# Experts half a step further behind the attention, first gate's sums by one-column matmuls, orders from token lists

## The chip, the cores and the metric

The kernel runs on one core of one Trainium2 chip. The metric is device time in microseconds (us) of one execution. Medians are over all timed runs of a kernel. A ratio is the mean time of one kernel's fast runs over the mean of the other's fast runs in the same rounds, so it is not quite the ratio of the medians. The profile of a kernel is one execution with the hardware profiler; its span is about 1.6 us shorter than the device time of the same run. The two executions compared stage by stage below, before and after, are both some 2 us slower than the medians of their kernels (241.70 against 239.66 us, 247.45 against 245.39).

Engine names in the profile: PE is TensorE, DVE VectorE, ACT ScalarE, POOL GpSimd, SP SyncE, which issues most loads and stores.

## The reference

Eight batches, eight heads, 576 positions, head size 64. Causal attention with a bias from a running sum of `s`; its output `x` (576 x 512 per batch) goes to a mixture of eight experts, of which one is chosen for a whole batch by the mean of `x`.

```python
scores = scale * np.matmul(q, k.transpose(0, 1, 3, 2))
cum = np.cumsum(np.maximum(s, 0.0), axis=-1)
bias = -(cum[:, :, :, None] - cum[:, :, None, :])
scores = np.where(causal, -1e9, scores + np.minimum(bias, 0.0))
attn = softmax(scores)                        # written out in the reference
x = np.matmul(attn, v)                        # then heads side by side: (8, 576, 512)
pooled = x.mean(axis=1)
logits = pooled @ w_gate                      # (8, 8)
e_idx = np.argmax(logits, axis=1)
h = np.maximum(x[mask] @ w1[e], 0.0)          # for each expert e and its batches
out[mask] = gate_w[mask, None, None] * (h @ w2[e])
```

The weights of an expert (two matrices of 512 x 1024) can be asked for only when the gate has chosen it.

## The kernel before

The attention is cut into 32 units of two heads, four to a batch. Two units share one load group of q, k and v. The experts' matmuls of a batch fill TensorE between the attention steps of later batches. The order on every engine is the order in which Python emits the instructions. Before, a hand-written function emits the start, and a loop with budgets the rest. The parts that matter:

```python
def load(n, after=None):          # SyncE's queue: q, k, and v in five pieces per group
    ...
def cast_qk(n, i):                # VectorE: q (i=0) or k (i=1) of group n to bf16
    ...
        nc.vector.tensor_copy(out=qk_bf[n][...], in_=src...)
def do_vS_pair(n, g):             # GpSimd: v of two heads, scaled by a column
    ...
    nc.gpsimd.tensor_tensor(out=dst[...], in0=src[...], in1=gc[...], op=ALU.mult)

def do_x(b, c):                   # transpose a quarter of x; copy it out with its sum
    ...
        nc.scalar.activation(out=xT[b][:, c, :], in_=flat, func=AF.Copy,
                             accum_out=pooled[b][:, c : c + 1])
    ...                           # or the same on VectorE; then gate_part(b, c - 1)

def do_gate(b):
    nc.tensor.matmul(lp, ones_sq, glog[b], start=True, stop=True)
    ...                           # VectorE: largest of eight, its index
    e_val = nc.gpsimd.value_load(idxc[0:1, 0:1], min_val=0, max_val=E - 1)
    picked[b] = nc.gpsimd.dma_start(out=w1, in_=moe_w1[e_val]...)
    nc.gpsimd.dma_start(out=w2, in_=moe_w2[e_val]...)

def begin():
    ...
    do_av_part(3, 0); do_av_part(3, 1)
    cast_qk(3, 0)
    do_tr_part(2, 1, 0, "a")
    for c in range(NC):
        do_x(0, c)
    do_tr_part(2, 1, 1, "a")
    do_gate(0)
    do_tr_part(3, 0, 0, "v")
    do_vS_pair(2, 0); do_vS_pair(2, 1)
    load(5, picked[0]); load(6)
    do_scores_masked(4, 0); exp_only(4, 0)
    do_gate2(0)
    cast_qk(3, 1)
    ...
    do_vS(3)
```

At the end `do_guard()` computes a flag on VectorE and TensorE (whether a general path is needed), every engine reads it and branches on it.

Of the kernel before, what the change touches and what calls it, by code (L numbers as in the profile page):

```python
# [9 lines left out]
FP32 = mybir.dt.float32  # L10
# [7 lines left out]
P = 128  # L18

# [248 lines left out]
def kernel(  # L268
# [11 lines left out]
    nc = tc.nc  # L280
# [36 lines left out]
    NQT, NPT, NVS, NVN = 2, 3, 2, 4  # L317
    NEARLY = 4
# [10 lines left out]

    def load_qk(n, i, after=None):  # L330
        b, Q = divmod(n, NQ)
        if i == 0:
            qk_nat[n] = nat.tile([P, 2, 2, R * D], FP32, name="qk_nat")
        ld = nc.sync.dma_start(
            out=qk_nat[n][:, i, :, :],
            in_=(q, k)[i][b, 4 * Q : 4 * Q + 4].rearrange(
                "(hh g) (p r) d -> (g p) hh (r d)", hh=2, p=64
            ),
        )
        if after is not None:  # L340
            tc.add_manual_dep(
                ld.ins, after.ins.name,
                mybir.DependencyInfo(mybir.DependencyClass.Sync, mybir.DependencyReason.DATA),
                reason="the weights of the chosen expert go first",
            )

    vS_done = set()

    def load_v(n, hh, eng=nc.sync):
        b, Q = divmod(n, NQ)  # L350
        assert n < NVN or n - NVN in vS_done
# [12 lines left out]
    def load(n, after=None):  # L364

        rest = n > 1 and after is None
        rest = rest and n > 2
        if n == 2:
            for m in range(2):
                for hh in range(5):  # L370
                    load_v(m, hh)
        if after is not None:
            for hh in (2, 3, 4):
                load_v(n - 1, hh)
        load_qk(n, 0, after)
        if rest:
            load_v(n - 1, 2)
            load_v(n - 1, 3)
        load_qk(n, 1)
        if rest:  # L380
            load_v(n - 1, 4)
        if n == NB - 1:
            for hh in range(5):
                load_v(n, hh)
        elif n > 1:
            load_v(n, 0)
            load_v(n, 1)

    def cast_qk(n, i):

        src = qk_nat[n][:, i, :, :]
        if n < NEARLY:
# [6 lines left out]
        if i == 0:  # L399
            qk_bf[n] = natb.tile([P, 2, R, 2, D], BF16, name="qk_bf")  # L400
# [11 lines left out]
    def do_tr_part(n, i, part, eng):  # L412
        r0, r1 = ((0, 5), (5, R))[part]
        tr = ps_mm.tile([P, 8, P], BF16, name="tr_ps", tag="mm_ps")
        for r in range(r0, r1):
            nc.tensor.transpose(tr[:, r - r0, :], qk_bf[n][:, i, r, :, :], ident_bf)  # L416
        o = tr_out(n, i, r0, r1)
        src = tr[:, 0 : r1 - r0, :].rearrange("p r (g n) -> p g n r", g=2)
        if eng == "v":
            nc.vector.tensor_copy(out=o, in_=src)  # L420
        else:
            nc.scalar.copy(out=o, in_=src)  # L422

    def do_tr(n, i):
        tr = ps_att.tile([P, 2, 8, P], BF16, name="tr_ps", tag="att_b")
        flat = tr.rearrange("p k r m -> p (k r) m")
        for r in range(R):
            nc.tensor.transpose(flat[:, r, :], qk_bf[n][:, i, r, :, :], ident_bf)  # L428
        j = 4 * n + 2 * i
# [4 lines left out]
        )  # L434

    def do_vS(n):
        b, Q = divmod(n, NQ)
        vS_done.add(n)
# [8 lines left out]
    def do_vS_pair(n, g):  # L447
        b, Q = divmod(n, NQ)
        src, dst = vN[n % NVN], vS[n % NVS]
        if g == 1:  # L450
            vS_done.add(n)
# [11 lines left out]
    def do_scores_half(u, half, alone=True):  # L463
        n, g = divmod(u, 2)
        src = qkT[n % NQT]
# [33 lines left out]
    def exp_only(u, half):  # L499
        ph = pT[u % NPT][:, 2 * half * HALF : 2 * (half + 1) * HALF]  # L500
        nc.scalar.activation(out=ph, in_=sc_ps[half], func=AF.Exp, scale=SCALE)  # L501
        return ph

    def do_exp(u, half):
        ph = exp_only(u, half)
# [12 lines left out]
    x_nat = {}  # L518

    def av_mm(u, hh, av):  # L520
        src = pT[u % NPT]
# [14 lines left out]
    def x_home(u):  # L536
        b = u // NC
        if b not in x_nat:
            x_nat[b] = xpool.tile([P, NT, H, D], BF16, name="x_nat", bufs=2)
        return x_nat[b], 4 * (u // 2 % NQ) + u % 2  # L540

    def do_av_part(u, hh):
        av = ps_mm.tile([P, NT, D + 1], FP32, name="av_ps", tag="mm_ps")
        av_mm(u, hh, av)
# [8 lines left out]
        )  # L553

    def do_av(u):
        av = ps_att.tile([P, 2, HALF], FP32, name="av_ps", tag="att_a")
        a4 = av[:, :, 0 : NT * (D + 1)].rearrange("p k (t d) -> p k t d", d=D + 1)
        for hh in range(2):
            av_mm(u, hh, a4[:, hh, :, :])
# [8 lines left out]
        )  # L568

# [3 lines left out]
    def do_x(b, c):  # L573
        if c == 0:
            xT[b] = xpool.tile([P, NC, S], BF16, name="xT", bufs=2)
            pooled[b] = small.tile([P, NC], FP32, name="pooled")
        src = x_nat[b].rearrange("p t h d -> p t (h d)")
        tr = ps_mm.tile([P, 8, P], BF16, name="x_ps", tag="mm_ps")
        for t in range(NT):
            nc.tensor.transpose(tr[:, t, :], src[:, t, c::NC], ident_bf)  # L580
        flat = tr.rearrange("p t n -> p (t n)")[:, 0:S]
        if c % 2 == 0 or b > 0:
# [8 lines left out]
        if c > 0:  # L591
            gate_part(b, c - 1)
        if c == NC - 1:
            gate_part(b, c)
# [6 lines left out]

    def gate_part(b, c):
        if c == 0:
# [10 lines left out]
    def do_gate(b):  # L614

        lp = ps_mm.tile([P, E], FP32, name="lg_ps", tag="mm_ps")
        nc.tensor.matmul(lp, ones_sq, glog[b], start=True, stop=True)  # L617
# [18 lines left out]
    def do_gate2(b):  # L636
# [12 lines left out]
    def do_mm1(b, sc, ft):  # L649
        if b not in hT:  # L650
            hT[b] = hpool.tile([P, NF, SP], BF16, name="hT")
        w1 = w_sb[b][0].rearrange("p c (m f) -> p c f m", f=NF)
        mm = ps_mm.tile([P, SC], FP32, name="mm_ps")
        for c in range(NC):
# [3 lines left out]
            )  # L658
        dst = hT[b][:, ft, sc * SC : (sc + 1) * SC]
        if RELU[ft] == "v":  # L660
            nc.vector.tensor_scalar_max(out=dst, in0=mm, scalar1=0.0)  # L661
        else:
            nc.scalar.activation(out=dst, in_=mm, func=AF.Relu)  # L663

    def do_mm2_tail(b, mm):
        w2 = w_sb[b][1]
        for fc in range(NF):
# [8 lines left out]
        o = opool.tile([P, Dm], FP32, name="o_sb")  # L676
        nc.scalar.mul(o[:, 0 : Dm // 2], mm[:, 0 : Dm // 2], gate[b])
        stores.append((b, NT - 1, TAIL, o))

    mm2_ps = {}  # L680
    stores = []

    def do_mm2(b, st, part):
        w2 = w_sb[b][1]
        n = min(P, S - st * P)
        if part == 0:
            mm2_ps[b, st] = ps_mm.tile([P, Dm], FP32, name="mm_ps")
        mm = mm2_ps[b, st]
        if st == NT - 1:
            do_mm2_tail(b, mm)  # L690
            return
        for fc in range(part * NF // 2, (part + 1) * NF // 2):
            nc.tensor.matmul(  # L693
                mm[0:n, :], hT[b][:, fc, st * P : st * P + n], w2[:, fc, :],
                start=(fc == 0), stop=(fc == NF - 1),
            )
        if part == 1:
            o = opool.tile([P, Dm], FP32, name="o_sb")
            if OEV[st] == "v":
                nc.vector.tensor_scalar_mul(out=o[0:n, :], in0=mm[0:n, :], scalar1=gate[b][0:n, :])  # L700
            else:
                nc.scalar.mul(o[0:n, :], mm[0:n, :], gate[b][0:n, :])  # L702
            stores.append((b, st, n, o))

    def do_store(all_=False):
        while stores and (all_ or len(stores) > 1):
            b, st, n, o = stores.pop(0)
            if st == NT - 1:
                for j in range(2):
                    nc.sync.dma_start(  # L710
                        out=out[b, st * P : st * P + n, j * Dm // 2 : (j + 1) * Dm // 2],
                        in_=o[j * 64 : j * 64 + n, 0 : Dm // 2],
                    )
                continue
            nc.sync.dma_start(out=out[b, st * P : st * P + n, :], in_=o[0:n, :])

    RELU = "avavavav"
    OEV = "aaaaa"

    def moe_quanta(b):  # L720
        q1 = [(1, partial(do_mm1, b, sc, ft)) for sc in range(2) for ft in range(NF)]
        q2 = [(1.76, partial(do_mm2, b, st, part)) for st in range(NT) for part in range(2)][:-1]

        return q1[0:9] + q2[0:2] + q1[9:11] + q2[2:4] + q1[11:] + q2[4:]


    s_nat = consts.tile([BH, S], FP32)
    nc.sync.dma_start(out=s_nat, in_=s.rearrange("b h i -> (b h) i"))
    for n in range(4):
        load(n)  # L730
    w_gate_sb = consts.tile([P, NC, E], FP32)
    nc.gpsimd.dma_start(out=w_gate_sb, in_=moe_w_gate.rearrange("(p c) e -> p c e", c=NC))

# [11 lines left out]
    )  # L745
    ones_sq = consts.tile([P, P], FP32)
# [21 lines left out]
    def do_gcol():  # L768
        g_ps = ps_mm.tile([P, NT, BH], FP32, name="mm_ps")
# [8 lines left out]
    NU = NC * B  # L778
    LAG = 7
    BEGIN = [LAG, LAG + 3] + [NC * b + LAG for b in range(2, B)]  # L780
    END = NU + LAG
    PRE = 3
    KEEP0 = 11

    def keep_pe(cnt):

        t = ps_mm.tile([P, 512], FP32, name="mm_ps")
# [3 lines left out]
    def early_max(n):  # L791
        nc.vector.tensor_reduce(
# [4 lines left out]
    def begin():  # L797
        keep_pe(KEEP0)
        cast_qk(0, 0)
        do_tr_part(0, 0, 0, "a")  # L800
        do_tr_part(0, 0, 1, "a")
        keep_pe(2)
        cast_qk(0, 1)
        do_tr_part(0, 1, 0, "v")
        do_gcol()
        do_tr_part(0, 1, 1, "a")
# [201 lines left out]
```

## Time and profile before

| before | value | how to read it |
|---|---|---|
| device time | 239.66 us, median of 3 (238.68 to 244.06) | later rounds on the other chips gave medians of 239.7 to 240.5 |
| span of the profile | 240.1 us, TensorE busy 214.1 | TensorE is the bound; its gaps are the question |
| gates (start of the gate matmul) | 27.11, 51.08, 80.58, 106.55, 132.30, 158.54, 183.38, 205.17 us | the distances are the periods |
| first expert matmul, last expert matmul's end | 39.41 and 233.69 us | between them TensorE is almost full |
| tail | 6.42 us | from the last matmul to the end |

To compare two kernels stage by stage I use one more mark: the first scores that follow the first attention product, at 16.37 us here. What comes before it is mostly the first loads, whose landing differs from run to run (the first q lands at 5.7 to 7.3 us in the fourteen profiles).

### The profile page before, as it was taken

Reading aid. Unit: us, or ns where it says so; the run is one execution under the profiler, and the core shown is the slowest. Engines: PE = TensorE matmul, PEld = TensorE weight load, DVE = VectorE, ACT = ScalarE, POOL = GpSimd, SP = SyncE. Lnnn points to the kernel's source line nnn. Section 1 sums busy time; section 2 is a strip of 40 time slices with the busy share of each in tenths; the row PEclk is TensorE's granted clock in tenths of the full one; section 3 lists DMA queues with packets and bytes.
Section 4 is the critical chain, followed back from the end, with each engine's and each line's share of the span. In section 5 each row is a group of like instructions: output and inputs, shape, how many; then the busy total and the mean of one; then the engine's idle time right before and its main releaser. Section 6 shows DMA issues by size and latency. Waiting matters only on the chain.

```text
span 240.1 us, 5998 instructions
## 1 busy us (share of the span) xinstructions
PE 214.1 (89%) x2330; PEld 157.1 (65%) x2330; DVE 164.5 (69%) x378; ACT 140.3 (58%) x254; POOL 92.6 (39%) x145
## 2 busy tenths in 40 slices
PE   6597789999999796999899997999999998898990
PEld 2365457875787655867597857776877776557740
DVE  5578768658797784779686875777777544396640
ACT  2588547467656745576648655685658675434330
POOL 6181092018845194308362556218360830100000
PEclk9999859999999999999999999999999999999997
DMA  5999999999999999999999999969921893399222
GB/s 174 342 237 351 306 200 216 344 309 284 221 309 312 286 257 209 304 306 305 225 254 347 313 217 241 337 159 187 228 94 44 162 230 117 67 214 235 82 84 76
DMA packets 55186, 55.14 MB, mean 230 GB/s; under 512 B 39712, under 2 KB 40752, under 8 KB 53104
## 3 DMA queue, kind: packets, MB, share of 16 engines
q1 hardware_dynamic: 52816, 37.91, 51.8%
q0 software_dynamic: 2336, 16.79, 35.4%
q8 instruction: 20, 0.33, 0.5%
q14 instruction: 14, 0.11, 0.2%
HBM read 62.03 MB, written 9.44 MB: 298 GB/s over the span
## 4 chain that ended last, share of the span: by engine, by line
PE 52%; DMA 26%; ACT 7%; DVE 7%; issue 4%; POOLq 1%; SPq 0%; ACTq 0%; POOL 0%; DVEq 0%
DMA w_sb<-in_moe_w_dram 24%; PE mm_ps L655 18%; PE mm_ps L693 13%; PE av_ps L528 6%; PE sc_ps L471 4%; ACT xT L583 4%; PE tr_ps L428 3%; DMA qk_nat<-in_k_dram 2%; ACT pT L501 2%; PE x_ps L580 2%; PE sc_ps L488 1%; PE tr_ps L416 1%; PE lg_ps L617 1%; PE mm_ps L669 1%; POOLq L624 1%
## 5 line engine op out<-in xcount | busy, mean ns | idle before, releaser
L655 PE MATMUL mm_ps<-xT,w_sb 128*128 128x288 bf16 x512 | 74.5, 289 | 4.9 <-DMA w_sb<-in_moe_w_dram 4.4
L501 ACT ACTIVATE pT<-sc_ps 128x1024 bf16<-128x1024 f32 x64 | 62.5, 1021 | 23.5 <-PE sc_ps L471 14.7
L655 PEld LDWEIGHTS <-w_sb 128*128 128x128 bf16 x512 | 61.5, 146 | 9.0 <-DMA w_sb<-in_moe_w_dram 5.1
L693 PE MATMUL mm_ps<-w_sb,hT 128*128 128x512 bf16 x256 | 64.9, 380 | 1.3 <-DMA w_sb<-in_moe_w_dram 0.6
L507 POOL TENSOR_SCALAR_AFFINE_SELECT pT<-pT 128x512 bf16<-128x512 bf16 x50 | 31.5, 638 | 43.8 <-ACT pT L501 43.7
L661 DVE TENSOR_SCALAR hT<-mm_ps 128x288 bf16<-128x288 f32 x64 | 28.7, 454 | 22.0 <-PE mm_ps L655 22.0
L663 ACT ACTIVATE hT<-mm_ps 128x288 bf16<-128x288 f32 x64 | 26.4, 413 | 26.8 <-PE mm_ps L655 26.1
L702 ACT ACTIVATE o_sb<-mm_ps,gw 128x512 f32<-128x512 f32 x32 | 22.1, 691 | 31.2 <-PE mm_ps L693 31.1
L693 PEld LDWEIGHTS <-hT 128*128 128x128 bf16 x256 | 22.8, 98 | 22.1 <-DVE hT L661 2.9
L430 DVE TENSOR_SCALAR_CACHE_REDUCE qkT<-tr_ps 128x1152 bf16<-128x1152 bf16 x24 | 32.5, 1353 | 3.8 <-PE tr_ps L428 3.6
L401 DVE TENSOR_SCALAR_CACHE_REDUCE qk_bf<-qk_nat 128x1152 bf16<-128x1152 f32 x24 | 32.1, 1342 | 0.0
L441 POOL TENSOR_TENSOR vS<-vN,g_col 128x1280 bf16<-128x1280 f32 x13 | 30.3, 2332 | 0.0
L626 POOL DMA_DIRECT2D w_sb<-in_moe_w_dram x8 | 5.2, 645 | 63.1 <-issue 18.7
L528 PEld LDWEIGHTS <-pT 128*128 128x128 bf16 x576 | 22.4, 99 | 4.7 <-ACT pT L501 1.4
L528 PE MATMUL av_ps<-vS,pT 128*128 128x65 bf16 x576 | 23.8, 195 | 1.1 <-ACT pT L501 0.9
L471 PE MATMUL sc_ps<-qkT 64*128 64x256 bf16 (+2 forms) x320 | 21.7, 256 | 1.8 <-ACT qkT L422 1.1
L563 DVE TENSOR_TENSOR x_nat<-av_ps,recip 128x640 bf16<-128x640 f32 x26 | 21.4, 824 | 0.9
L583 ACT ACTIVATE xT<-x_ps 128x576 bf16<-128x576 bf16 x30 | 19.2, 650 | 3.4 <-PE x_ps L580 3.0
L471 PEld LDWEIGHTS <-qkT 64*128 64x128 bf16 x320 | 12.6, 95 | 11.2 <-issue 3.9
L428 PE MATMUL tr_ps<-ident_bf,qk_bf 128*128 128x128 bf16 x216 | 16.0, 219 | 0.1
L428 PEld LDWEIGHTS <-qk_bf 128*128 128x128 bf16 x216 | 13.9, 98 | 3.1 <-DVE qk_bf L401 0.5
L561 DVE RECIPROCAL recip<-av_ps 128x10 f32<-128x10 f32 x26 | 5.7, 220 | 14.0 <-PE av_ps L528 12.9
(92 smaller groups left out, 187.8 us busy)
## 6 DMA issues: line engine op xcount, KB each, us to landing
w_sb<-in_moe_w_dram POOLq DMA_DIRECT2D x16, 1024.0 KB, 12.4
qk_nat<-in_q_dram SPq DMA_DIRECT2D x16, 576.0 KB, 5.6
qk_nat<-in_k_dram SPq DMA_DIRECT2D x16, 576.0 KB, 6.3
vN<-in_v_dram SPq DMA_DIRECT2D x64, 128.0 KB, 5.5
out_dram<-o_sb SPq DMA_DIRECT2D x32, 256.0 KB, 5.7
vN<-in_v_dram SPq DMA_DIRECT2D x16, 64.0 KB, 5.8
out_dram<-o_sb SPq DMA_DIRECT2D x16, 64.0 KB, 4.2
s_nat<-in_s_dram SPq DMA_DIRECT2D x1, 144.0 KB, 2.8
```

Of the source, the lines that this page charges most:

```text
L401: nc.vector.tensor_scalar(out=qk_bf[n][:, i, :, :, :].rearrange("p r hh d -> p hh r d"), in0=src.rearrange("p hh (r d) -> p hh r d", d=D), ...
L428: nc.tensor.transpose(flat[:, r, :], qk_bf[n][:, i, r, :, :], ident_bf)
L430: nc.vector.tensor_scalar(out=tr_out(n, i, 0, R), in0=flat[:, 0:R, :].rearrange("p r (g n) -> p g n r", g=2), scalar1=1.0, scalar2=0.0, op ...
L441: nc.gpsimd.tensor_tensor(out=dst[:, :, :, 0:D], in0=src, in1=gc[:, :, :, None].to_broadcast([P, NT, 4, D]), op=ALU.mult,)
L471: nc.tensor.matmul(sc[:, hh, o : o + W[tj]], src[hh * 64 : hh * 64 + 64, 1, g, tj * P : tj * P + P], src[hh * 64 : hh * 64 + 64, 0, g, tj ...
L501: nc.scalar.activation(out=ph, in_=sc_ps[half], func=AF.Exp, scale=SCALE)
L507: nc.gpsimd.affine_select(out=ap, in_=ap, compare_op=ALU.is_ge, fill=0.0, base=0, pattern=[[0, 4], [1, P]], channel_multiplier=-1,)
L528: nc.tensor.matmul(av[:, ti, :], src[:, o : o + P], vs[:, tj, 2 * hh + u % 2, :], start=(tj == tjs[0]), stop=(tj == tjs[-1]),)
L583: nc.scalar.activation(out=xT[b][:, c, :], in_=flat, func=AF.Copy, accum_out=pooled[b][:, c : c + 1])
L655: nc.tensor.matmul(mm, w1[:, c, ft, :], xT[b][:, c, sc * SC : (sc + 1) * SC], start=(c == 0), stop=(c == NC - 1),)
L661: nc.vector.tensor_scalar_max(out=dst, in0=mm, scalar1=0.0)
L693: nc.tensor.matmul(mm[0:n, :], hT[b][:, fc, st * P : st * P + n], w2[:, fc, :], start=(fc == 0), stop=(fc == NF - 1),)
```

## The change

Its intent: the experts of a batch start half a step later, so that more work stands between a gate and the first matmul that needs its weights; the first gate gets its sums of x from matmuls with a column of ones straight after the attention, without waiting for the x transposes and their copies; and every engine's order comes from lists of tokens, tuned by hand at the fine joints. One token is one helper call: `C3.1` casts k of group 3, `v2.0` scales half of the v of group 2, `V3` all of group 3, `l3.4` loads a v piece, `G0 m0` are the first gate's matmul and pick, `D` is the guard.

```diff
+BEGIN = """
+k2 k11 C0.0 U0.0.0 u0.0.0.1 ... C1.0 v0.0 v0.1 l3.2 L4.0 l3.3 L4.1 l3.4 l4.0 l4.1 U1.0.0 ...
+... B2.0 b2.0 B2.1 b2.1 N0 n0 N1 n1 M3.1 E3.1
+U2.0.0 u2.0.0.1 U2.0.1 u2.0.1.1 C2.1 B3.0 b3.0 B3.1 b3.1 N2 N3 n2 n3 X0.0 x0.0.1 G0 m0 C3.0 X0.1
+U2.1.1 u2.1.1.1 x0.1.0 X0.2 x0.2.1 U2.1.0 u2.1.0.1 l4.4 X0.3 x0.3.0 U3.0.0 u3.0.0.0 v2.0 v2.1
+l4.2 l5.0 l5.1 l4.3 W5.0 l6.1 M4.0 g0 L5.1 l5.3 L6.0 l5.4 L6.1 E4.0 l6.0 l5.2 C3.1 U3.0.1
+u3.0.1.0 M4.1 E4.1 U3.1.0 u3.1.0.1 U3.1.1 u3.1.1.0 V3 M5.0 ...            (cut)
+"""
+PERIOD = ...   # one batch's tokens, played four times, shifted by one batch
+FINISH = """   ... Y7.3.0 Y7.3.1 y7.3.1 Z7 y7.4.2 O7.3 O7.4.2 D
+"""
-    def begin():  ...          # and the loop with budgets
-    def do_x(b, c):
+    def x_mm(b, c):            # every helper split into its TensorE part and its way out
+    def x_out(b, c, eng):
+        if b == 0:             # first batch: a plain copy, no sum
+            ...
+    w_gate_n = consts.tile([P, NC, E], FP32)
+    nc.scalar.dma_start(out=w_gate_n, in_=moe_w_gate.rearrange("(c p) e -> p c e", p=P))
+    def sum_mm(j):             # the sums of 128 channels over 576 positions
+        for ti in range(NT):
+            nc.tensor.matmul(t, src[0:n, ti, j * P : (j + 1) * P], ones_bf[0:n, :],
+                             start=(ti == 0), stop=(ti == NT - 1))
```

The sums come out with channels in another order than the old ones, so the gate's table is loaded a second time (`w_gate_n`). In the old order the guard stood inside the last second-layer product, `Y7.3.0 D Y7.3.1`.

## The prediction

> **What bounds the kernel now.** I read the page first, then the PE waits, then the timeline at each of those waits, then the chain, then the end of the span.
>
> ```profile
> PE 214.1 (89%) x2330; PEld 157.1 (65%) x2330; DVE 164.5 (69%) x378; ACT 140.3 (58%) x254; POOL 92.6 (39%) x145
> ...
> PE   6597789999999796999899997999999998898990
> ...
> PEclk9999859999999999999999999999999999999997
> DMA  5999999999999999999999999969921893399222
> ```
>
> PE is the bound: 26 us of its span are idle, and they lie in a few places. From 0 to 38 us it is 6 to 9 tenths busy. The clock row falls to 8 and 5 tenths around 24 to 36 us. Between 38 and 234 us PE is nearly full, with dents. The last 6.4 us have no matmul. These are the dents:
>
> ```profile
> PE mm_ps L655 <- DMA w_sb<-in_moe_w_dram: 4.4, 4, 2.1
> PE lg_ps L617 <- DVE glog L609: 3.0, 3, 1.4
> PE x_ps L580 <- DVE x_nat L563: 0.7, 1, 0.7
> PE sc_ps L471 <- DVE qkT L430: 0.6, 2, 0.4
> PE mm_ps L693 <- DMA w_sb<-in_moe_w_dram: 0.6, 1, 0.6
> PE mm_ps L693 <- DVE hT L661: 0.3, 1, 0.3
> ```
>
> That view covers 37 to 234 us and sums to 9.6 us; half is the first expert matmul of a batch waiting for weights that were asked for only when the gate had chosen the expert. The timeline gives the places:
>
> ```profile
> 80.58 0.39 PE L617 MATMUL lg_ps<-glog,ones_sq 128*128 128x8 f32 x2 [1.37 <-DVE glog L609]
> 94.08 1.20 PE L655 MATMUL mm_ps<-xT,w_sb 128*128 128x288 bf16 x8 [2.06 <-DMA w_sb<-in_moe_w_dram]
> 119.83 1.20 PE L655 MATMUL mm_ps<-xT,w_sb 128*128 128x288 bf16 x8 [0.84 <-DMA w_sb<-in_moe_w_dram]
> 146.07 1.20 PE L655 MATMUL mm_ps<-xT,w_sb 128*128 128x288 bf16 x8 [1.33 <-DMA w_sb<-in_moe_w_dram]
> ```
>
> Gate to weights takes 13.45 us for batch 2 (80.58 to 94.03). By the same reading of the chain it is 13.2 us for batch 3 and 13.7 us for batch 4. Batches 5 and 6 do not wait, because the loads are over and the DMA row falls to 6 tenths and below. The steady period between gate matmuls is 25.75 us (gate 3 to 4), 26.24 us (4 to 5) and 24.84 us (5 to 6); the last has no weight wait and is the floor of this order.
>
> The first gate is slow too, and the end of the span holds a wait that is not on the page's engine rows:
>
> ```profile
> 27.11 0.36 PE L617 MATMUL lg_ps<-glog,ones_sq 128*128 128x8 f32 x2 [1.50 <-DVE glog L609]
> ...
> L976 PEldq COMPARE_BRANCH  x1: 4102/4102/4102, 233.7 to 233.7; - x1
> L976 SPq COMPARE_BRANCH  x1: 50/50/50, 236.5 to 236.5; - x1
> ```
>
> The second pair is the branch on the guard's flag (whether the general path runs). PE's takes 4.10 us, from 233.7 to 237.8. It costs nothing now, since SP waits for the last store until 237.88 anyway and then needs 2.2 us to the end.
>
> [...] Here PE idles 0.69 and 1.50 us around the first gate among short transposes, and the clock drops for about 6.8 us[...]. [...] the chain gives it, 10.64 us from issue to landing for batch 2, of which the 2.1 MB read as f32 would take 7 us alone at the profile's 298 GB/s.
>
> **The change part by part.** Order alone carries no new bytes. I rebuilt both kernels' instruction orders and compared them engine by engine. Unit costs on PE, from start to start in the chain: one expert step H (4 matmuls of 288 columns) 0.49 us, half a second-layer tile Y 0.86, a tail Z 0.99, scores S 0.55, attention-value A 0.55, transposes T 0.50, one x transpose 0.28.
>
> 1. Start. Before, the first gate needs four x transposes, four evacuations with sums (0.65+0.20 us each on ACT, 0.75+0.08 on DVE) and four gate sums. Now sums of x come from 4 groups of 5 one-column matmuls; I take each as a transpose-like 0.06 to 0.1 us, for its weight load, so 0.3 to 0.5 us a group. Two groups come before attention unit 3 and delay it by up to 0.8 us less one filler; two follow it. Last x slice ready 23.9 us, + 0.8 delay + 0.5 (last group) + 0.5 (two DVE steps) + 0.1 = 25.8 against 27.1. First weights then land at 36.6 instead of 37.9. [...] But ACT must still do the x copies, two qkT copies and seven exponentials of 1.02 us before unit 7, about 11 us from 25.3, so the first expert starts near 37 to 38.5 instead of 39.4. Gain 1.5 us (0.5 to 2.5).
>
> 2. Batch 2. After its gate, PE now has 5H+5Y+2S+3A+2T+Z = 11.5 us of work before its first expert matmul, against 4H+4Y+3S+2A+2T+Z = 10.2. The gate's own wait shrinks because a score and a Y half (1.4 us) stand before it: 1.37 to about 0.8. A new wait of about 1 us appears at unit 14's scores, which now follow their transposes after 0.5 us while DVE needs 1.35. Together: 2.0 us gained.
>
> 3. Batches 3 to 6. After the gate PE has 6H+5 or 6Y+3S+3A+2T+Z, about 13.4 us, against 11.5 before (12.0 measured with joints, so 14.0 now). Weights need 13.2 and 13.7, so both waits go: 0.84 and 1.33. The 0.27 us joint at L693 <- DVE hT in each period goes too. The x transposes get new small waits (0.2 and 0.3 us, PSUM buffers freed by ACT in order) in place of the old 0.29 and 0.18. Period 24.5 us: 1.2 + 1.7 + 0.3 = 3.2 us gained.
>
> 4. DVE. Per period three 512-column evacuations and one x evacuation move to it (3 x 0.69 + 0.83) and three hT ones leave (3 x 0.45): 19.3 + 1.5 = 20.9 us of 24.5. It stays under PE.
>
> 5. Batch 7. The x wait (0.65) goes, as three H stand there. The gate's wait grows from 1.45 to about 2 us, since DVE carries hT and two x evacuations in series. The wait for second weights (0.65, at 221.8) goes, as 17.8 us of work stands behind the gate where 15.4 stood. The guard's transposes leave the middle of the last tile (0.4). Sum 1.8 us with joints.
>
> 6. Tail. The guard now comes last on DVE and PE. From the last matmul, T: evacuation to T+0.5, guard's first DVE part 0.8, transposes 0.7, second part 1.3, flag read 0.5: T+4.0. PE's branch of up to 4.1 us then starts after, not before, the stores: T+8.2, and 1.0 us to the end, T+9.2. SP's way: flag ready T+3.5, read and checked 1.1, at least 0.5 past the branch, 2.2 to the end as now, so T+7.3 at the earliest. Now it is T+6.4. Cost 1.0 to 2.8 us, taken as 2.0. Splitting the last store over two queues saves 0.5 us that no longer sets the end.
>
> Sum: 1.5 + 2.0 + 3.2 + 1.8 + 0.1 (batch 1) - 2.0 = 6.6 us off 239.66, so 233.0 us.
>
> **The rivals.** (a) The weights merely wait elsewhere: loads are regrouped, DMA is full until 145 us, and a gate that comes sooner meets the same queue. For it: 10.6 us under load against 8.3 to 8.7 for batches 5 to 7. Against: the extra 1.9 us of work exceeds the wait. If weights took 2 us more, steps 2 and 3 lose 3 us: 236. (b) DVE or ACT becomes the bound through in-order evacuation: DVE at 85% of a period with 4 PSUM buffers leaves little slack. Half a us per period and some at the ends: 236 to 238. (c) The tail eats more or nothing: [...] if it is the whole 4.1 us, 234. (d) Fine-grained orders remove joints that my sums leave alone, and the clock stays up at the start: 229 to 231.
>
> **Range and chances.** 233.0 us, 229.0 to 237.0 eight times in ten. Two per cent is 234.9. The centre is beyond it by 1.9 us with a spread of about 3, and a deliberate order is more likely to help than my added waits: faster 0.70, same 0.27, slower 0.03.
>
> **What would show it.** Step 1: first gate matmul near 25.8 us, first expert matmul at 37 to 38.5, clock slices without a 5. Step 2 and 3: PE <- DMA w_sb waits under 1.5 us in sum, gate-to-gate periods near 24.5 us. Step 4: DVE about 21 us per period. Step 5: gate 7 still waits about 2 us for DVE. Step 6: span minus last expert matmul 7.3 to 9.2 us, with PE's branch after the guard. Periods above 25.2 us, or new PE waits on DVE over 3 us in sum, would prove the sum wrong; so would a tail still at 6.4.

## The result, and the profile after

The changed kernel took 245.39 us (median of 4, 245.27 to 247.45) against 239.73 (4 runs, 238.68 to 244.06) in the same rounds: ratio 1.027, interval 1.021 to 1.033. It is slower. All runs of the changed kernel were in the fast state.

Stage by stage, in us, from the two traces:

| stage | before | after | after less before | predicted |
|---|---|---|---|---|
| start to the mark | 16.37 | 16.39 | 0.0 | 0 |
| mark to second gate | 34.71 | 43.38 | +8.7 | -1.6 |
| second gate to last gate | 154.09 | 148.47 | -5.6 | -5.2, and a part of step 5 |
| last gate to last matmul | 28.52 | 28.56 | 0.0 | the rest of step 5's -1.8 |
| tail | 6.42 | 8.99 | +2.6 | +2.0 |
| span | 240.1 | 245.8 | +5.7 | -6.6 |

The middle did nearly what was hoped. The whole loss is in the start, and a smaller one in the tail. The rows of the page of the changed kernel that answer to the first fence of the prediction:

```profile
PE 213.9 (87%) x2326; PEld 159.9 (65%) x2350; DVE 173.8 (71%) x392; ACT 130.0 (53%) x238; POOL 90.9 (37%) x145
...
PE   7787773599899897999999999999999997999950
...
PEclk9999998589999999999999999999999999999997
DMA  5999999984999969999999999999940992597140
```

A slice is 6.1 us. TensorE does the same work (213.9 us busy), but slices 7 and 8 (37 to 49 us) are 3 and 5 tenths busy, and the clock falls to 5 tenths in and behind the hole (in the trace it is at half from 40.8 to 51.0 us). From 49 us on there are hardly any dents. The waits of TensorE from 48 to 238 us (waited for; us in total, times, longest) no longer hold one for expert weights:

```profile
PE sc_ps L567 <- DVE qkT L518: 1.6, 2, 1.4
PE lg_ps L784 <- DVE glog L746: 1.6, 1, 1.6
PE tr_ps L511 <- DVE qk_bf L471: 0.9, 1, 0.9
```

Before, `w_sb` stood at the top of that view with 4.4 us. The same view from 20 to 48 us shows the new ones:

```profile
PE av_ps L633 <- POOL vS L537: 7.0, 1, 7.0
PE tr_ps L490 <- DVE early L463: 2.6, 1, 2.6
```

In the timeline of TensorE of the changed kernel (start, us, engine, line, operation; in brackets the idle time before it and what ended it):

```profile
25.03 0.39 PE L784 MATMUL lg_ps<-glog,ones_sq 128*128 128x8 f32 x2
...
32.19 0.68 PE L490 MATMUL tr_ps<-ident_bf,early 128*128 128x128 bf16 x9 [2.61 <-DVE early L463]
...
45.80 1.15 PE L633 MATMUL av_ps<-vS,pT 128*128 128x65 bf16 x18 [6.96 <-POOL vS L537]
46.76 5.43 PE L831 MATMUL mm_ps<-xT,w_sb 128*128 128x288 bf16 x26
```

The gate came 2.1 us sooner than before (27.11), as it should. The first expert matmul came 7.4 us later (39.41 before). Between them stand two waits, one for GpSimd and one for VectorE.

**The long wait.** GpSimd's timeline of the changed kernel:

```profile
27.61 0.59 POOL L797 DMA_DIRECT2D w_sb<-in_moe_w_dram  x1 [8.78 <-DVE xT L717]
...
28.89 1.27 POOL L549 TENSOR_TENSOR vS<-vN,g_col 128x640 bf16<-128x640 f32 x1
...
30.26 1.25 POOL L549 TENSOR_TENSOR vS<-vN,g_col 128x640 bf16<-128x640 f32 x1
43.20 2.33 POOL L533 TENSOR_TENSOR vS<-vN,g_col 128x1280 bf16<-128x1280 f32 x1 [11.69 <-DMA vN<-in_v_dram]
```

The scaling of group 3's v (`V3`) waited 11.7 us for a v piece. SyncE issued that piece, `l3.4`, at 26.81 us, 0.8 us ahead of the weights. The trace records its landing in sixteen shares, which I take for one share per DMA engine (the page counts 16). Fifteen of them had landed by 32.6 us; the last landed at 43.04, and the last packet of the weights ended at 42.59. In the kernel before, the piece was issued at 25.96 us and landed at 32.06, with the weights issued only at 29.67, and GpSimd did the same scaling at 34.07 without a wait:

```profile
34.07 2.33 POOL L441 TENSOR_TENSOR vS<-vN,g_col 128x1280 bf16<-128x1280 f32 x1
```

The kernel before had trapped pieces too: the v pieces issued at 28.75 and 31.00 us landed at 44.48 and 44.83, but nothing waited for them. What the change moved is which piece is in the trap.

The view of the DMA of the changed kernel from 33 to 41 us (queue: packets, MB, share of the 16 engines' time; then the issues of the window, with the median time to landing) shows what the piece was up against; the v pieces it lists are later ones, the last of them issued at 28.99 us:

```profile
q0 software_dynamic: 214, 1.62, 96.8%
q1 hardware_dynamic: 214, 0.05, 5.0%
...
vN<-in_v_dram SPq DMA_DIRECT2D x2, 128.0 KB, 5.3
vN<-in_v_dram SPq DMA_DIRECT2D x1, 64.0 KB, 14.9
```

q0 carries the weights, q1 everything of SyncE. Both moved 214 packets, and in each of the eight microseconds the two counts differ by at most one (22 to 36 packets each): the engines took one of each in turn. A packet of the weights is 8 KB and took 624 ns in the trace, one of v is 256 bytes and took 31 (medians; 16 of the 214 on q0 carry 4 bytes). So q1 had half of the turns and a thirtieth of the bytes. The piece, 64 KB in packets of 256 bytes, has 16 packets for each engine if the shares are equal. My estimate for an engine that has all 16 left when the weights arrive is 16 x 0.65 = 10.4 us, and the difference between 32.6 and 43.0 is as much. The packed trace does not keep which engine a packet ran on, so that the late engine had all of them left is inferred.

**The short wait.** A cast on VectorE, of k of group 3, in the changed kernel (second line; the first is the q cast just ahead of it):

```profile
26.15 0.74 DVE L463 CAST early<-qk_nat 128x1152 bf16<-128x1152 f32 x1
28.56 3.57 DVE L463 CAST early<-qk_nat 128x1152 bf16<-128x1152 f32 x1
```

and the same cast in the kernel before:

```profile
29.93 0.74 DVE L394 CAST early<-qk_nat 128x1152 bf16<-128x1152 f32 x1
```

The same work took 3.57 us instead of 0.74. In the changed kernel it lay beside GpSimd's two scalings (28.89 to 31.51 us) and ended 0.6 us after them. Before, GpSimd was issuing the weights during the cast and scaled afterwards. In GpSimd's timelines, the weight issue during which the cast starts, before and then changed:

```profile
29.67 1.12 POOL L626 DMA_DIRECT2D w_sb<-in_moe_w_dram  x1 [10.57 <-DVE qkT L420]
28.20 0.54 POOL L799 DMA_DIRECT2D w_sb<-in_moe_w_dram  x1
```

Before, it was thus the issue that took longer (1.12 us, where the median of the eight is 0.58). In all five traces in which the cast starts 0.24 to 0.27 us into a weight issue (before, e4, e7, e8, e10 below), that issue takes 1.1 us and the cast 0.74; in the three in which it starts 0.35 to 0.37 us into one (changed, e1, e2), the issue takes 0.54 and the cast waits for all the scalings. About a tenth of a microsecond separates the two groups. Which was first in the changed kernel the trace does not settle: the cast is recorded at 28.56 us, inside GpSimd's second weight issue (28.20 to 28.74) and ahead of its first scaling (28.89). Nor does it show by what means the one holds the other; it shows the two times, 0.74 against 3.57 us.

**The tail.** The branch on the guard's flag, in the view of its source line (engine, operation, count, duration in ns, first and last start):

```profile
L1020 SPq COMPARE_BRANCH  x1: 50/50/50, 241.0 to 241.0; - x1
...
L1020 PEldq COMPARE_BRANCH  x1: 3582/3582/3582, 241.1 to 241.1; - x1
```

The guard's last VectorE step ended at 240.46 us, 3.7 us after the last expert matmul; then TensorE's branch took 3.58 us. The stores had landed by 239.8. So the guard and the branch set the end, where before the last store did.

### The profile page after: what moved, and what is told of

Same layout as the page of the kernel before. It is cut to its first block, busy times and chain, and to the rows that moved or that the text cites. A ratio compares the mean times of both kernels' runs of the same rounds, so it can differ in the third digit from the quotient of the medians.

```text
span 245.8 us, 6001 instructions
## 1 busy us (share of the span) xinstructions
PE 213.9 (87%) x2326; PEld 159.9 (65%) x2350; DVE 173.8 (71%) x392; ACT 130.0 (53%) x238; POOL 90.9 (37%) x145
## 3 DMA queue, kind: packets, MB, share of 16 engines
q0 software_dynamic: 2336, 16.79, 34.6%
## 4 chain that ended last, share of the span: by engine, by line
PE 68%; DVE 11%; DMA 9%; ACT 3%; issue 3%; SPq 2%; POOL 1%; ACTq 0%; DVEq 0%
PE mm_ps L831 23%; PE mm_ps L863 20%; PE av_ps L633 6%; DMA vN<-in_v_dram 6%; PE sc_ps L567 6%; PE tr_ps L511 4%; PE x_ps L708 3%; DVE x_nat L684 3%; PE mm_ps L892 3%; DMA qk_nat<-in_k_dram 2%; ACT pT L599 2%; DVE qkT L518 2%; DVE qk_bf L471 1%; POOL vS L533 1%; SPq L446 1%
## 5 line engine op out<-in xcount | busy, mean ns | idle before, releaser
L831 PE MATMUL mm_ps<-xT,w_sb 128*128 128x288 bf16 x512 | 77.0, 295 | 0.0
L831 PEld LDWEIGHTS <-w_sb 128*128 128x128 bf16 x512 | 62.5, 147 | 5.3
L863 PE MATMUL mm_ps<-w_sb,hT 128*128 128x512 bf16 x234 | 59.2, 379 | 1.2 <-issue 0.2
L841 ACT ACTIVATE hT<-mm_ps 128x288 bf16<-128x288 f32 x77 | 29.7, 415 | 38.1 <-PE mm_ps L831 37.1
L606 POOL TENSOR_SCALAR_AFFINE_SELECT pT<-pT 128x512 bf16<-128x512 bf16 x50 | 31.5, 638 | 38.5 <-ACT pT L599 38.4
L863 PEld LDWEIGHTS <-hT 128*128 128x128 bf16 x256 | 23.5, 98 | 22.3 <-issue 1.1
L843 DVE TENSOR_SCALAR hT<-mm_ps 128x288 bf16<-128x288 f32 x51 | 22.3, 451 | 18.8 <-PE mm_ps L831 18.8
L533 POOL TENSOR_TENSOR vS<-vN,g_col 128x1280 bf16<-128x1280 f32 x13 | 30.4, 2337 | 11.7 <-DMA vN<-in_v_dram 11.7
L633 PEld LDWEIGHTS <-pT 128*128 128x128 bf16 x576 | 22.4, 98 | 11.7 <-issue 6.7
L797 POOL DMA_DIRECT2D w_sb<-in_moe_w_dram x8 | 4.6, 577 | 61.7 <-issue 21.1
L879 ACT ACTIVATE o_sb<-mm_ps,gw 128x512 f32<-128x512 f32 (+1 forms) x25 | 15.6, 628 | 12.5 <-PE mm_ps L863 7.8
L719 ACT ACTIVATE xT<-x_ps 128x576 bf16<-128x576 bf16 x21 | 13.5, 649 | 7.1 <-PE x_ps L708 7.1
L881 DVE TENSOR_SCALAR o_sb<-mm_ps,gw 128x512 f32<-128x512 f32 x14 | 10.4, 744 | 9.5 <-PE mm_ps L863 9.5
```

Source lines behind the costliest of these rows:

```text
L533: nc.gpsimd.tensor_tensor(out=dst[:, :, :, 0:D], in0=src, in1=gc[:, :, :, None].to_broadcast([P, NT, 4, D]), op=ALU.mult,)
L606: nc.gpsimd.affine_select(out=ap, in_=ap, compare_op=ALU.is_ge, fill=0.0, base=0, pattern=[[0, 4], [1, P]], channel_multiplier=-1,)
L633: nc.tensor.matmul(av[:, ti, :], src[:, o : o + P], vs[:, tj, 2 * hh + u % 2, :], start=(tj == tjs[0]), stop=(tj == tjs[-1]),)
L831: nc.tensor.matmul(mm, w1[:, c, ft, :], xT[b][:, c, sc * SC : (sc + 1) * SC], start=(c == 0), stop=(c == NC - 1),)
L841: nc.scalar.activation(out=dst, in_=mm, func=AF.Relu)
L863: nc.tensor.matmul(mm[0:n, :], hT[b][:, fc, st * P : st * P + n], w2[:, fc, :], start=(fc == 0), stop=(fc == NF - 1),)
```

## The experiments

Theory: (1) the early weights trap the v piece, (2) the cast is blocked by GpSimd's scaling, (3) the late guard lengthens the tail. The rival to (1) and (2) is that only the half step and the other new orders make the start later. Twelve kernels ran. Every edit is to the changed kernel unless said otherwise, and all gave correct results. This table is from their profiles, in us:

| run | time, median | ratio to before | mark | mark to 2nd gate | 2nd to last gate | last gate to last matmul | tail |
|---|---|---|---|---|---|---|---|
| before | 239.7 | | 16.4 | 34.7 | 154.1 | 28.5 | 6.4 |
| after | 245.4 | 1.027 | 16.4 | 43.4 | 148.5 | 28.6 | 9.0 |
| e1_v3_first | 244.4 | 1.020 | 17.1 | 39.5 | 148.5 | 28.6 | 9.1 |
| e2_guard_early | 240.6 | 1.000 | 17.2 | 36.9 | 148.5 | 29.0 | 6.2 |
| e3_gate_late | 239.9 | 0.998 | 18.6 | 33.6 | 148.5 | 28.6 | 9.1 |
| e4_old_start | 241.5 | 1.004 | 18.2 | 35.5 | 149.0 | 28.6 | 9.1 |
| e5_late_guard | 237.2 | 0.988 | 18.8 | 33.7 | 148.5 | 29.0 | 6.1 |
| e6_v3_cast | 240.5 | 1.002 | 19.0 | 33.2 | 150.1 | 28.6 | 9.3 |
| e7_before_list | 242.2 | 1.010 | 19.4 | 33.8 | 152.9 | 28.6 | 6.6 |
| e8_before_sums | 240.7 | 1.002 | 18.1 | 34.2 | 151.7 | 28.4 | 6.5 |
| e9_late_table | 237.3 | 0.987 | 16.1 | 36.3 | 148.1 | 29.0 | 6.2 |
| e10_before_table | 240.1 | 1.002 | 16.5 | 33.8 | 153.0 | 28.4 | 6.4 |
| e11_table_mid | 238.4 | 0.996 | 16.7 | 35.6 | 148.1 | 29.0 | 5.9 |
| e12_gate_early | 237.9 | 0.988 | 16.5 | 33.1 | 151.1 | 29.0 | 6.1 |

The kernel before had medians of 240.3, 239.9, 240.5 and 240.5 in the four calls. The middle columns hardly move between kernels of one order; the differences lie in the start and the tail.

**e1_v3_first: all of group 3's v pieces are issued ahead of the next q and k.**

```diff
-l3.2 L4.0 l3.3 L4.1 l3.4 l4.0
+l3.2 l3.3 l3.4 L4.0 L4.1 l4.0
```

> The changed kernel, with the last three v pieces of head group 3 issued before the q and k loads of group 4 instead of between them; nothing else. My theory: the 7.0 us wait of unit 6's attention-value matmul on vS is one v piece caught behind the first batch's weights (one of its 16 DMA engines finishes at 43.04 us, the other 15 by 32.6). If so the piece lands before 31 us, the wait is gone, the first expert matmul starts at about 39.3 instead of 46.8 us, the clock does not fall after it, and the time is 237 us (235.5 to 238.5). Rival: GpSimd, or the long 3.57 us DVE cast beside it, holds unit 6 back: then the wait stays and the time is 245.

Measured 244.4 us (243.87 to 247.26), ratio 1.020 (1.012 to 1.029): a miss by 7 us. The trapped piece itself is freed: the last v piece landed at 29.0 us, and GpSimd scaled group 3 at once:

```profile
32.17 2.32 POOL L533 TENSOR_TENSOR vS<-vN,g_col 128x1280 bf16<-128x1280 f32 x1
```

But now this third scaling follows the first two directly, and the cast on VectorE was held for all three:

```profile
29.24 5.87 DVE L463 CAST early<-qk_nat 128x1152 bf16<-128x1152 f32 x1
```

TensorE waited 4.9 us for the cast instead of 2.6, and its clock was at half from 34.6 to 41.4 us. So the second cause took over a good part of the first. This is the best evidence that the scalings hold the cast: two scalings give 3.57 us, three give 5.87, none gives 0.74. In both long cases the cast ended 0.6 us after the last scaling.

**e2_guard_early: the guard back inside the last product.**

```diff
-Y7.3.0 Y7.3.1 y7.3.1 Z7 y7.4.2 O7.3 O7.4.2 D
+Y7.3.0 D Y7.3.1 y7.3.1 Z7 y7.4.2 O7.3 O7.4.2
```

> The changed kernel with the guard put back where it was, between the halves of the last but one output tile. My theory: PE's branch on the guard's flag takes 3.6 us because it comes after everything else, and sets the end; put back, the tail after the last expert matmul shrinks from 9.0 to 6.4 us, PE gives 0.4 us back before it, and the time is 243.2 us (242.5 to 244). Rival: the stores or the end of the program set the tail: then no change, 245.4.

Measured 240.6 us (239.09 to 244.23; the highest counts as slow), ratio 1.000 (0.991 to 1.010). The tail is 6.2 us, as expected. The total fell further than expected, because the start, although its order is untouched, was 6.4 us shorter than in the changed kernel's profile: the trapped piece landed at 39.2 us this time instead of 43.0, its scaling began at 39.4, and TensorE did not wait for it. So the trap cost less in this profile. I take it that fewer packets were left when the weights came, but that isn't shown, and it isn't plain scatter either: the changed kernel's five runs all lie between 245.27 and 247.45 us, e2's fast ones, on another chip, between 239.09 and 241.68. How much of the 4.8 us is the guard is therefore read from the tail (2.8 us) and from e5, not from this total. The cast took 3.57 us again.

**e3_gate_late: the gate's matmul and pick back behind the four x transposes.**

```diff
-X0.0 x0.0.1 G0 m0 C3.0 X0.1 ... X0.3 x0.3.0 U3.0.0
+X0.0 x0.0.1 C3.0 X0.1 ... X0.3 x0.3.0 G0 m0 U3.0.0
```

> The changed kernel with the first gate's matmul and choice put back behind all four x transposes, so the weights are asked for 1.5 to 2 us later; the load order stays the changed one. If the early request for weights is what catches the v piece, the wait of unit 6 is gone or under 1 us and the time is 237.5 us (236 to 239). If the load order alone is at fault (the piece is issued 0.85 us later than before), the wait stays at 5 us or more and the time is 243 to 246.

Measured 239.9 us (239.47 to 240.26), ratio 0.998 (0.993 to 1.004). Two tokens, moved back, take away 5.5 us (medians of different calls). The cast is short again, and the scaling of group 3 does not wait. VectorE's timeline:

```profile
31.04 0.73 DVE L463 CAST early<-qk_nat 128x1152 bf16<-128x1152 f32 x1
```

and GpSimd's:

```profile
35.57 2.33 POOL L533 TENSOR_TENSOR vS<-vN,g_col 128x1280 bf16<-128x1280 f32 x1
```

A later gate gives a sooner second gate: 33.6 us from the mark instead of 43.4. The rival falls: the other new orders of the start are all still there. The total was 2.4 us above the expectation; the mark lay at 18.6 us instead of 16.4.

**e4_old_start: the whole start of the kernel before (its copies with sums too), the rest as changed.**

```diff
-FIRST, BEGIN up to C4.1 k6 as changed; x copies of batch 0 without sums
+the same stretch in the order before; x copies of batch 0 with sums
```

> The changed kernel with the whole start up to attention unit 7 in the order of before (loads, gate sums from the x copies), the rest as changed. This is the half step and the new orders of the experts alone. By the stretches of the trace (gate 2 to gate 7 saves 5.6 us, the tail costs 2.6) it should take 236.5 us (235 to 238), with the first expert at 39.4 us. If it takes 239 or more, the gain of the periods needs the late start and is not real.

Measured 241.5 us (240.0 to 242.55), ratio 1.004 (0.997 to 1.011): a miss by 5 us. No trap and no long cast in its trace, so the cause of the large loss is where e3 put it. The long tail was already in the expectation. Against the profile of before, the trace shows 1.8 us of the miss ahead of the mark (18.2 against 16.4 us) and 0.8 between the mark and the second gate; the middle is 149.0 us, 0.5 more than in the changed kernel. The rest is not traced; the profile of before is itself of a slow execution. By its own words the expectation ("239 or more") would make the gain of the periods unreal. The trace says otherwise: with the old start the middle still takes 149.0 us against 154.1, so the test by the total was badly set.

**e5_late_guard: e3 and e2 together.**

> The changed kernel with the first gate matmul back behind the four x transposes (as in e3) and the guard's work back inside the last second-layer product (as in e2). If the early gate and the late guard are two separate costs, they add: e3's 239.9 us less the 2.8 us of shorter tail = 237.1 us (236.3 to 237.9), tail 6.2 us, H0 to G1 10.96 us. If e2's lower time was only a luckier start and the tail is hidden anyway, it stays at 239.9 us. It would be the first version to beat the kernel before, by 1.1 to 1.3%.

Measured 237.2 us (235.55 to 240.47, 6 runs; the highest counts as slow), ratio 0.988 (0.982 to 0.993). The two costs add, as the theory said. This version beats both kernels: before by 1.2%, and the changed one by 3.3%, from the medians of different calls. In the view of the branch's line, TensorE's branch now starts ahead of the last stores (issued at 230.5 and 231.0 us), as before the change:

```profile
L1020 PEldq COMPARE_BRANCH  x1: 3985/3985/3985, 230.0 to 230.0; - x1
```

It ends at 234.0 us, and the last store's wait on SyncE at about the same time.

**e6_v3_cast: the early gate stays, with both traps taken away.**

```diff
-l3.2 L4.0 l3.3 L4.1 l3.4 l4.0
+l3.2 l3.3 l3.4 L4.0 L4.1 l4.0
-G0 m0 C3.0 X0.1 ... l5.2 C3.1 U3.0.1
+G0 m0 C3.0 C3.1 X0.1 ... l5.2 U3.0.1
```

> The changed kernel with the gate left early, but group 3's v pieces issued before the next group's q (as in e1) and group 3's k cast moved ahead of GpSimd's scaling of the v's (right behind the q cast). Theory [...]: the cast takes 0.75 us again instead of 5.87, TensorE's 4.9 us wait for it and the half-clock stretch after it are gone, and the time falls from e1's 244.4 us by about 5 to 239.2 us (238 to 240.5). Rival (the early weights starve everything behind them, so another wait takes the place of the cast's): over 242 us, with a new TensorE wait of several us between 30 and 45 us.

Measured 240.5 us (239.6 to 241.77), ratio 1.002 (0.995 to 1.008), 3.9 us under e1. Both casts together took 1.41 us, and neither wait is left: 33.2 us from the mark to the second gate, against 39.5 in e1. The total is 1.3 us above the expectation, at the edge of its range. In the profile, of a run of 241.8 us, one period is 25.8 us instead of 24.2 (third gate to fourth), with the clock at half from 88.7 to 92.1 us; why it fell there, in this run alone, I can't say.

**e7_before_list: a control, the whole order of before as token lists.** The instruction sequences are those of before but for one memset and the load of `w_gate_n`, which nothing uses.

> Control: the whole order of the kernel before, written as token lists of the changed kernel (same instruction sequence on every engine but one more memset and one more small load). Expected within 0.3% of the kernel before, 239.5 to 240.5 us. It gives a trace of the order before beside those of the experiments. If it is over 1% from it, how the order is written down would matter, against all theories.

Measured 242.2 us (240.95 to 243.97), ratio 1.010 (1.003 to 1.017). This was not expected. Its mark lies at 19.4 us, 3 us later than before's. The first q landed at 7.06 us (6.43 before), and TensorE's clock was at half from 10.1 to 16.9 us. After the mark nothing is lost. The new load consists of 512 packets of 32 bytes and runs while the first q comes in, so I suspected it.

**e8_before_sums: the order of before with only the new sums (`N`, `n` in place of `P0`).**

```diff
-b2.1 ...  b3.1 ...  x0.1.0 P0.0 ... P0.3
+b2.1 N0 n0 N1 n1 ...  b3.1 N2 N3 n2 n3 ...  x0.1.0 ...
```

> The order before with only the gate sums changed: one-column matmuls with ones behind the attention of the first batch in place of the accumulating copies, the gate matmul left at its place in the order. Theory: the 1.66 us wait of TensorE before the gate matmul goes, some 1.0 us of new waits for x_nat at the sums come, so the gate comes 0.5 to 1 us sooner and the first expert hardly, as the rest of the start is dense: 239.3 to 240.3 us. If the sums alone bring the trapped v piece or the long cast, it would be over 242 us. The prediction's step 1 (gain passes on to the first expert) would give about 238.8 us.

Measured 240.7 us (238.76 to 241.26), ratio 1.002 (0.995 to 1.009). That is 0.4 us above the range, with the mark at 18.1 us. The sums alone bring neither trap and gain nothing in time: the first gate is 10.1 us behind the mark instead of 10.7, the second gate no sooner than in e7 and e10.

**e9_late_table: e5, with the second table issued by GpSimd at about 16 us.**

```diff
-    nc.scalar.dma_start(out=w_gate_n, in_=...)      # at 0.95 us
+    (in do_vS_pair, behind the scaling of v0.1)  nc.gpsimd.dma_start(out=w_gate_n, in_=...)
```

> e5 with the second copy of the gate's table (512 packets of 32 bytes on ScalarE's queue, issued at 0.95 us) issued by GpSimd behind its second scaling instead, at about 16 us. Theory (these packets go between those of the first q and hold it up): the first q lands at about 6.4 us instead of 7.3, the scores' marker (first scores behind the first attention product) comes at 16.4 to 17.5 us instead of 18.8, and the time falls from 237.2 by 1 to 2 us, to 235.7 us (235 to 236.5). Rival (the first loads only land differently from run to run, whatever the table does): 237.2 us, marker between 17 and 19.

Measured 237.3 us (236.02 to 238.62, 6 runs), ratio 0.987 (0.982 to 0.993), as e5: a miss, at the rival's number. The first q did land sooner (5.74 us) and the mark is at 16.1. But the table took 7.2 us to land, with the DMA row at 9 tenths (2.7 us in e11, issued at 11.1), and was itself waited for by VectorE, on the way to the gate, so nothing was left of the gain:

```profile
23.11 0.24 DVE L774 TENSOR_SCALAR glog<-w_gate_n,sum_ps 128x8 f32<-128x8 f32 x1 [1.85 <-DMA w_gate_n<-in_moe_w_gate_dram]
```

**e10_before_table: the control e7, with the table's load moved in the same way.**

> The control e7 (order before, with the unused second table) with the table's load moved in the same way. Theory: it comes back to the kernel before, 239.5 to 240.2 us, 2 us under e7's 242.2. Rival (run-to-run, or something else of the rewriting costs): stays at 241.5 to 242.5 us.

Measured 240.1 us (239.51 to 242.46, 6 runs), ratio 1.002 (0.996 to 1.008), mark at 16.5 us, as expected. So the early table may cost some 2 us in the order of before (242.2 against 240.1), but the two come from different calls and the intervals of their ratios overlap (1.003 to 1.017, 0.996 to 1.008). The fourteen profiles together say a little more. In the nine with the early table the first q lands at 6.4 to 7.3 us and the mark lies at 16.4 to 19.4; in the five without it, at 5.7 to 6.5 and 16.1 to 16.7. The six marks of 18 us and more all belong to traces in which TensorE's clock was at half for 3.4 to 6.8 us ahead of the mark (e3, e5 to e8) or reached full speed only at 10.9 us (e4; by 7.3 us in the others).

**e11_table_mid: e5, with the table issued by GpSimd at about 11 us.** **e12_gate_early: the same, with the gate early and both traps taken away as in e6.**

> e5 with the second table's load issued by GpSimd between its first two scaling instructions, at about 10.5 us: behind the first q and k, and 5 us sooner than in e9, where VectorE waited 1.85 us for it. Theory (the table costs where its packets or its arrival meet something that is waited for): the first q lands by 6.5 us, no wait for the table, marker to first gate 10.4 us as in e5, and 1 to 2 us off e5 and e9: 235.6 us (234.8 to 236.6), ratio to before about 0.98. Rival (the place of the table is noise): 237.2 us as e5 and e9.

> The same, but with the gate as early as the change has it, group 3's v pieces ahead of the next q and its k cast ahead of the scaling (e6), so with every trap found taken away. If an early gate is worth something by itself (the prediction's step 1: 1.5 us), it beats e11 by over 1 us; if the start is TensorE's dense work and not the gate (theory, from e6 against e3: marker to second gate 33.2 against 33.6 us), it is within 0.7 us of e11.

e11 measured 238.4 us (236.9 to 240.51, 6 runs), ratio 0.996 (0.990 to 1.002); e12 237.9 us (236.44 to 244.22, 6 runs, the two highest in the slow state), ratio 0.988 (0.980 to 0.995). e11 misses: its mark is at 16.7 us, but with the start ahead of time and the gate late, the first expert matmul now waits for its weights:

```profile
41.28 0.96 PE L833 MATMUL mm_ps<-xT,w_sb 128*128 128x288 bf16 x6 [1.40 <-DMA w_sb<-in_moe_w_dram]
```

In e12 the gate is early enough for that: 33.1 us from the mark to the second gate, 2.5 less than e11. So in this pair of profiles an early gate is worth something once its traps are gone and the loads are on time. Whether it is in time stays open: by the fast runs alone e12 is 1.1 us under e11 (means 237.2 and 238.4), by the medians 0.5, and the intervals of the ratios overlap. The profiled execution of e12 ended no sooner (span 235.8 against 235.3 us), since it lost 3.0 us between its third and fourth gates (27.2 us instead of 24.2). On TensorE:

```profile
98.25 0.53 PE L833 MATMUL mm_ps<-xT,w_sb 128*128 128x288 bf16 x3 [2.79 <-ACT o_sb L881]
```

and on ScalarE, whose copy out of PSUM waited for a free output buffer:

```profile
97.73 0.47 ACT L881 ACTIVATE o_sb<-mm_ps,gw 128x256 f32<-128x256 f32 x1 [3.80 <-DMA out_dram<-o_sb]
```

The store that held the buffer was issued just behind a batch's weights. The DMA view of e12 from 84 to 92 us shows the same alternation as above:

```profile
q0 software_dynamic: 216, 1.64, 99.0%
q1 hardware_dynamic: 225, 0.05, 5.3%
...
out_dram<-o_sb SPq DMA_DIRECT2D x1, 256.0 KB, 12.2
...
out_dram<-o_sb SPq DMA_DIRECT2D x2, 64.0 KB, 13.8
```

What was won at one gate was lost, in this profile, at the queue of another: the stores that stood behind 2 MB of weights took 12.2 and 13.8 us.

## Why the prediction was wrong

**Step 1 failed**: "Gain 1.5 us (0.5 to 2.5)". Its first half was right: the gate came at 25.03 us (predicted 25.8). It then let the weights pass 1.3 us sooner (it read their landing in the kernel before as 37.9 us; the trace has 38.36) and named ScalarE's work as the only other limit of the first expert matmul. It did not ask what sooner weights do to the transfers beside them, nor what GpSimd, freed sooner by the pick, would run beside. Both are visible in the profile of before, had I looked there: the v piece landed only 2.4 us after the weights were issued, the cast ended 0.8 us ahead of GpSimd's first scaling (30.67 and 31.48 us), and it had already drawn a weight issue out to 1.12 us. The first expert matmul came at 46.76 us instead of 37 to 38.5, and the stage lost 8.7 us where 1.6 were to be gained. That is 10.3 of the 12.3 us between the predicted and the measured change of the span. e3 shows the cause (gate alone moved back: -5.5 us), e1 and e6 its two parts. The weights themselves landed 0.7 us sooner (37.7 against 38.4), for a gate 2.1 us sooner. With both traps gone the stage took 33.1 to 33.2 us, against 34.7 in the profile of before and 33.8 in its two controls: a gain of 1.5 us against the one and 0.6 against the others, so the predicted size is at the upper end of what was there, and it had to be made room for. Its sign "clock slices without a 5" failed too: the clock was at half for 10.2 us, in and behind the hole of 7.0. In the kernel before, the clock dropped without any such hole: from 20 us to the drop at 28.4, TensorE was busy for 5.6 of 8.4 us and its longest wait was 1.5. What lowers it is not shown.

**Steps 2 and 3** held. Step 2 said 2.0 us for batch 2; third gate to fourth went from 25.97 to 24.21 us, 1.8 gained. The waits for the weights (2.06 us) and at the gate (1.37) went; a new wait of scores for VectorE came, 1.36 us where about 1 was forecast. Step 3 said a period of 24.5 us; it is 24.65, three times over, and no wait for weights is left. The three periods gained 2.9 us of 3.2.

**Step 4** held: VectorE is busy 20.5 us per period (predicted 20.9).

**Step 5** was half right. The last gate waits 1.58 us (predicted about 2). From the seventh gate to the last matmul the time went from 50.31 to 49.41 us, 0.9 gained of 1.8; the last stretch from gate to end was not shorter at all.

**Step 6** held in kind and was somewhat small: the tail is 8.99 us (predicted 7.3 to 9.2), the cost 2.6 us where 2.0 were taken. e2 and e5 show that it is the guard's place: 6.1 to 6.2 us with the guard inside the last product, at the price of 0.4 us there.

**The rivals.** Rival (a) had the right idea, "a gate that comes sooner meets the same queue", but put it at batches 2 to 6 and let it cost the weights. It was the other transfers that paid, in the start, and in e12 between the third and fourth gates. Rivals (b) and (d) play no part in the loss. Rival (c) is answered: the branch takes 3.6 us, at the end of the span where nothing hides it.

**What stays open.** Two controls in different calls suggest a cost of the early second table (2.1 us), and the marks of the fourteen profiles point the same way, but moving it gained nothing in the changed order, where other waits came up (e9, e11). And the changed kernel's own profile had the mark at 16.4 us with the early table, so the table does not delay the start every time. Why single stretches run at half clock in some runs (e6, e7), and why e2's trapped piece came free sooner, is not settled either.

## What to carry to other kernels

Before a large transfer is issued sooner, list the small transfers that will still be in flight and ask what each is needed for: here, on DMA engines that were 97% busy with weights, they got every second turn and almost none of the bytes (0.05 MB against 1.62), and single transfers of 64 to 256 KB issued just behind 2 MB of weights took 12.2 to 15.5 us to land (changed kernel, e2, e12). Let what is needed soon land first, or be issued well ahead. And when an engine is freed sooner, look at what it will now run beside (a cast of 0.74 us took 3.57 beside two scalings): two parts of a tuned order can be apart for a reason that no comment tells.
